# The gelu's VectorE work dealt over three steps, and waits of the heads' normalisation that pass in any step

## The chip, the cores and the metric

The kernel runs on 1 core of one Trainium2 chip. The metric is the device time of one execution in microseconds (us); of several executions the median is given. Lower is better.

## The reference, cut to what matters

One transformer block in its parallel form: with x of 2048 tokens by 640 channels and xn = layernorm(x),

```python
def _A_ref(x, wqkv, wo):            # 32 heads of 20 channels
    q, k, v = qkv of x @ wqkv
    p = softmax(q @ k.T * 20 ** -0.5)
    return (p @ v) @ wo
def _B_ref(x, w1, b1, w2, b2):
    y = _layernorm(x)
    h = gelu(y @ w1 + b1)           # tanh form, 1536 wide
    return h @ w2 + b2
return x + _A_ref(xn, wqkv, wo) + _B_ref(xn, w1, b1, w2, b2)
```

## The kernel before, in words

**Three stretches.** First the input is normalised, transposed and split into pairs of 16-bit numbers, and q, k and v are made (lines 162 to 590, to about 225 us of the trace). Then comes the long stretch of attention with the MLP woven in (to about 1260 us). The rest is the output projection.

**The attention stretch.** A pair of heads `g` and a half `hf` of the queries make one of 32 units, in the order of the list ORDER. A unit has two column blocks `cc` of 512 queries, and each of these runs over 16 key blocks `kb` in four groups of four (GRP). For each key block `scores` (line 674) makes two matmuls into a PSUM tile `s` (three buffers) and ScalarE's exp from there into a tile `p` (L682). For two of the four key blocks of a group, `rest` (line 689) lets VectorE write `low`, what `p` loses when it is cut to 16 bits (L694). Once per group `pv` (line 699) multiplies the tiles of the group *before* with the values: four matmuls per split block with the cut `p`, then four with the two `low` tiles of that group, then eight with the two whole tiles, all on L711. So the second `low` of a group is asked for by TensorE one group later.

**The fill.** Between the scores of key blocks 1 and 2 of each group, `other` (line 1062) puts some matmuls of the MLP: `layer1` (L913) makes a 128 by 2 by 256 tile `pu` of the hidden layer, `layer2` (L945) a tile `py` of the output. Both use the one buffer of the pool `psM`, so the next tile of either kind waits until VectorE has read the one before. The projection (L1024) follows the MLP in the same way.

**Steps.** What is to be done beside this on the other engines is written as generators, and `tick` (line 611) takes each one step further. `tick` is called twice per group, after the scores of key blocks 1 and 3. There are two lists. Each generator in `sides` goes on at every step: a gelu, an `addup`, the loads of the next unit's q and k (`load_stack`). Those in `patient` go on only when the step has no VectorE work of the others in it: a generator yields the VectorE work that it has just issued, in us, `tick` adds it up in `t`, and `if its is patient and t > 0: break` skips the whole list. `begin` runs a generator's first part at once, at the place where the fill has ended a tile, and its work counts for the next step.

**The gelu** (line 845), 48 times: at `begin` it reads `pu` from PSUM (L849) and adds the bias (L850). At the next step come a square (L853) and a multiply-add (L854), then a step with nothing, then tanh on ScalarE (L857), then three VectorE instructions at the fourth step (L859 to L861) that write `hT`.

**The heads' normalisation** (`finish`, line 764), twelve times: when two or three units of the same half are unloaded, the sums and the unnormalised outputs come back from DRAM into `lt` and `oa` (L774, L802). VectorE adds and inverts the sums (L810 to L817), they go out and come back spread over the heads as `rb` (L831). Then VectorE adds, multiplies, cuts and subtracts on `oa` (L835, L837, L839, L841), one instruction a step, and the result goes out (L842). This is done for two blocks of 512 columns, with bare `yield`s as waits for the transfers in between. All but those of the last groups of heads in the second half stand in `patient`, as does `scale_ahead` (line 871), which waits eight steps and then scales a row.

In each step, the generators in `sides` come first, then `patient`, and after the step VectorE gets the next `low`: the first `low` of a group after the step behind key block 1, the second after the step behind key block 3.

Of the kernel before, what the change touches and what calls it, by code (L numbers as in the profile page):

```python
# [42 lines left out]
def mha_mlp_kernel(tc, x, wqkv, wo, w1, b1, w2, b2, out):  # L43
# [4 lines left out]
    with (  # L48
# [544 lines left out]
        with ExitStack() as scope:  # L593
# [4 lines left out]

            sides, patient = [], []
            taken = [0.0]

            def begin(it):
# [6 lines left out]
            def tick():  # L611
                t, taken[0] = taken[0], 0.0
                for its in (sides, patient):
                    if its is patient and t > 0:
                        break
                    for it in list(its):
                        r = next(it, self_end)
                        if r is self_end:
                            its.remove(it)
                        else:  # L620
                            t += r or 0.0

# [113 lines left out]
            def dma(g, hf):  # L736

                return (nc.scalar if (g, hf) == ORDER[-1] else nc.sync).dma_start

            def unload(g, hf, ev):  # L740
# [9 lines left out]
                if g + 1 in ENDS:  # L750
                    fins.append(finish(g + 1 - UNITS[ENDS.index(g + 1)], g + 1, hf))
                    if len(fins) == 1:

                        (sides if hf == 1 and g + 1 >= TAIL else patient).append(finishing())

            fins, direct = [], []
            ready = [0, 0]

            def finishing():
                while fins:  # L760
                    yield from fins[0]
                    fins.pop(0)

            def finish(g0, g1, hf):
                nh, r0, r1 = 2 * (g1 - g0), 2 * g0 * DH, 2 * g1 * DH
                last = (g1 - 1, hf) == ORDER[-1]
                go = dma(g1 - 1, hf)
                w = 1024 if last else 512
                lt = m1.tile([P, 2, 64], F32, tag="lt", name="lt")
                n = checks.pop()  # L770
                yield
                gd = g1 - 1 if last else g1
                for p in range(2):
                    go(lt[: (gd - g0) * 32, p, :], lpart[p, hf, 2 * g0 : 2 * gd, :].rearrange("h (b t) -> (h b) t", t=64))  # L774
                    for a in range(2 if last else 0):

                        r = 64 * a + PAD + DH + VW * p
                        go(lt[(nh - 2 + a) * 16 : (nh - 1 + a) * 16, p, :],
                           direct[0][r : r + 1].rearrange("o c (b t) -> o (c b) t", t=64))
                for c0 in range(0, 1024, w):  # L780
                    cols = slice(hf * 1024 + c0, hf * 1024 + c0 + w)
                    if last:
                        o0, o1 = (ptp.tile([P, 2, 512], F32, tag="p", name="oa").rearrange("p c t -> p (c t)")
                                  for _ in range(2))
                        rb = o0

                        sel = [ptp.tile([P, 2, 512], F32, tag="p", name="sel").rearrange("p c t -> p (c t)")
                               for _ in range(2)]
                        for b0, t in zip((0, 8), sel):
                            nc.gpsimd.tensor_copy(  # L790
                                t[: nh * 16, : 8 * nh * DH].rearrange("p (b h d) -> p b h d", b=8, h=nh),
                                ident[: nh * 16, : nh * 16].rearrange("p (h b) -> p b h", b=16)[:, b0 : b0 + 8, :, None]
                                .to_broadcast([nh * 16, 8, nh, DH]))
                    else:
                        o = m1.tile([P, 2, 512], F32, tag="oa", name="oa")
                        o0, o1 = o[:, 0], o[:, 1]
                        rb = m1.tile([P, 512], F32, tag="rb", name="rb")
                    hl = o1.bitcast(F16).rearrange("p (s t) -> p s t", s=2)[: r1 - r0]
                    o0, o1, rb = o0[: r1 - r0], o1[: r1 - r0], rb[: r1 - r0]
                    rd = 2 * gd * DH - r0  # L800
                    for p, o in enumerate((o0, o1)):
                        go(o[:rd], opart[p, r0 : r0 + rd, cols])  # L802
                        for a in range(2 if last else 0):
                            q0 = 64 * a + PAD + VW * p
                            go(o[rd + a * DH : rd + (a + 1) * DH], direct[0][q0 : q0 + DH].rearrange("d c t -> d (c t)"))
                    if c0 == 0:
                        for _ in range(W1 if last else 4):
                            yield
                        l = lt[: nh * 16]
                        nc.vector.tensor_add(l[:, 0], l[:, 0], l[:, 1])  # L810

                        nc.vector.tensor_scalar(l[:, 1], l[:, 0], LO, None, ALU.is_ge, ALU.min,
                                                accum_out=good[: nh * 16, n : n + 1])
                        if not last:
                            yield
                        nc.vector.tensor_scalar(l[:, 0], l[:, 0], 1e-30, None, ALU.max)
                        nc.vector.reciprocal(l[:, 1], l[:, 0])  # L817
                        if not last:
                            go(linv[hf, 2 * g0 : 2 * g1, :].rearrange("h (b t) -> (h b) t", t=64), l[:, 1])
                        for _ in range(4 if last else 1):  # L820
                            yield
                    if last:

                        rb = psS.tile([P, 2, 512], F32, tag="s", name="rb")[: nh * DH]
                        for b in range(16):
                            nc.tensor.matmul(rb[:, b // 8, b % 8 * 64 : b % 8 * 64 + 64],
                                             sel[b // 8][: nh * 16, b % 8 * nh * DH : (b % 8 + 1) * nh * DH],
                                             l[:, 1], start=True, stop=True)
                        rb = rb.rearrange("p c t -> p (c t)")
                    for h in range(0 if last else nh):  # L830
                        go(rb[h * DH : (h + 1) * DH],  # L831
                           linv[hf, 2 * g0 + h : 2 * g0 + h + 1, c0 : c0 + w].to_broadcast([DH, w]))
                    for _ in range(W2 if last else 4):
                        yield
                    nc.vector.tensor_add(o0, o0, o1)  # L835
                    yield
                    nc.vector.tensor_mul(o0, o0, rb)  # L837
                    yield
                    nc.vector.tensor_copy(hl[:, 0], o0)  # L839
                    yield  # L840
                    nc.vector.tensor_sub(hl[:, 1], o0, hl[:, 0])  # L841
                    go(oscr[:, r0:r1, cols].rearrange("s d t -> d s t"), hl)  # L842
                ready[hf] += 1

            def gelu(ps, r2f, hT, f):
                u = m1.tile([P, 2, MC], F32, tag="u", name="u")
                w = m1.tile([P, 2, MC], F32, tag="w", name="w")
                scale_rows(r2f)
                nc.vector.tensor_mul(u, ps, r2f[:, None, :].to_broadcast([P, 2, MC]))  # L849
                nc.vector.tensor_add(u, u, b1t[:, f : f + 2, None].to_broadcast([P, 2, MC]))  # L850
                yield 1.2

                nc.vector.tensor_mul(w, u, u)  # L853
                nc.vector.scalar_tensor_tensor(w, w, 1.0 / 0.044715, u, ALU.add, ALU.mult)  # L854
                yield 1.2
                yield
                nc.scalar.activation(w, w, AF.Tanh, scale=0.7978845608028654 * 0.044715)  # L857
                yield
                nc.vector.scalar_tensor_tensor(u, w, 1.0, u, ALU.add, ALU.mult)  # L859
                nc.vector.tensor_scalar(hT[:, f : f + 2, 0, :], u, ch, None, ALU.mult)  # L860
                nc.vector.scalar_tensor_tensor(hT[:, f : f + 2, 1, :], u, ch, hT[:, f : f + 2, 0, :],  # L861
                                               ALU.mult, ALU.subtract)
                yield 1.7

            def scale_rows(r2f):

                if r2f in unscaled:
                    unscaled.remove(r2f)
                    nc.vector.tensor_scalar(r2f, r2f, f1, None, ALU.mult)

            def scale_ahead(r2f):
                for _ in range(8):
                    yield
                scale_rows(r2f)

            def addup(ps, xb, t0, hf):
# [121 lines left out]
            W1, W2 = 12, 9  # L998
# [56 lines left out]
            with tc.manual_schedule():  # L1055
# [18 lines left out]
                for g, hf, cc, kb0 in groups:  # L1074
# [23 lines left out]
                    if cc == 0 and kb0 == 0 and (g, hf) != ORDER[-1]:  # L1098
                        n = ORDER[ORDER.index((g, hf)) + 1]
                        sides.append(load_stack(*n, *([stacks[g, hf][1]] if n[0] == g else [])))  # L1100
                n = 0
# [119 lines left out]
```

## Time and profile before

| | us |
|---|---|
| median of 3 executions | 1363.1 (1362.19 to 1364.39) |
| the profiled execution's own time | 1364.71 |
| its span, from the first to the last instruction | 1363.0 |
| VectorE busy | 1060.5 |
| ScalarE busy | 1129.6 |
| mean granted TensorE clock | 0.998 |

The span is what the trace shows of one execution; 1.7 us of the device time lie around it. Busy times are unions over an engine's instructions. A wait in the trace is idle time of an engine just before an instruction, with the instruction or transfer that came last before it could start. A TensorE instruction's end is modelled, so idle time of TensorE is read with care. In rows of the timeline the columns are start, time from the first start to the last end, engine, line, operation, tiles and count; in square brackets stands the idle time before it and what ended it. VectorE is DVE there, TensorE PE, ScalarE ACT, and SPq is the queue from which SyncE issues transfers.

### The profile page before, as it was taken

The numbers are of one execution on the slowest core, as the hardware profiler recorded it, in microseconds if no ns is written. First come the engines' busy times: TensorE is split into PE (matmuls) and PEld (weight loads), VectorE is DVE, ScalarE is ACT, GpSimd is POOL, SyncE is SP. The second block draws the span as 40 slices with busy tenths as digits, with TensorE's granted clock in tenths as the row PEclk, the third lists the DMA queues.
The fourth block names the chain that finished last, engine by engine and source line by source line (L and its number), as shares of the span: only waits on it lengthen the run. The fifth ranks groups of instructions, "written<-read, shape, count | busy, mean of one in ns | idle before, by whom it ended". The sixth has DMA issues, their size and how long they took to land.

```text
span 1363.0 us, 29029 instructions
## 1 busy us (share of the span) xinstructions
PE 1335.1 (98%) x11651; PEld 591.6 (43%) x11651; DVE 1060.5 (78%) x1436; ACT 1129.6 (83%) x1305; POOL 30.2 (2%) x74
## 2 busy tenths in 40 slices
PE   9999999999999999999999999999999999999998
PEld 6545545443334334433433343434433333333465
DVE  6658835998779897978797789897879898888732
ACT  6654525999999999999999999999999999999700
POOL 2000000000000000000000000000000000000000
PEclk9999999999999999999999999999999999999999
DMA  9868731111113221212321141223032223244275
GB/s 269 270 157 154 146 101 57 34 52 43 48 58 94 62 83 60 52 50 84 93 71 51 37 109 48 86 62 86 19 87 85 70 81 86 59 135 118 88 233 175
DMA packets 103073, 127.94 MB, mean 94 GB/s; under 512 B 27516, under 2 KB 69568, under 8 KB 102932
## 3 DMA queue, kind: packets, MB, share of 16 engines
q1 hardware_dynamic: 99864, 119.60, 31.2%
q0 software_dynamic: 2304, 5.24, 2.4%
q8 instruction: 93, 1.52, 0.5%
q10 hardware_dynamic: 764, 1.18, 0.3%
q14 instruction: 48, 0.39, 0.1%
HBM read 80.50 MB, written 42.51 MB: 90 GB/s over the span
## 4 chain that ended last, share of the span: by engine, by line
PE 79%; DVE 9%; ACT 7%; issue 3%; DMA 2%; ACTq 0%; SPq 0%; DVEq 0%
PE o L711 26%; PE s L680 17%; PE py L945 11%; PE pu L913 9%; PE qkp L322 8%; PE vp L395 5%; ACT p L682 4%; PE z L1024 4%; DVE low L694 3%; DMA oa<-ev 1%; DVE u L849 1%; DMA qkscr<-qkhl 1%; DVE u L850 1%; DVE w L853 1%; DVE w L854 1%
## 5 line engine op out<-in xcount | busy, mean ns | idle before, releaser
L682 ACT ACTIVATE p<-s 128x1024 f32<-128x1024 f32 x1024 | 972.3, 1041 | 43.4 <-PE s L680 37.0
L694 DVE TENSOR_TENSOR low<-p 128x1024 f16<-128x1024 f32 x512 | 610.7, 1219 | 159.9 <-ACT p L682 159.7
L711 PE MATMUL o<-p,vfull 128*32 128x512 bf16 (+1 forms) x4096 | 430.8, 493 | 0.0
L680 PE MATMUL s<-qs,ks 61*128 61x512 f16 x2048 | 316.5, 382 | 7.4 <-ACT p L682 6.5
L680 PEld LDWEIGHTS <-ks 61*128 61x128 f16 x2048 | 63.7, 94 | 293.6 <-issue 291.3
L913 PE MATMUL pu<-xm,w1t 128*128 128x256 f16 x1440 | 179.3, 274 | 1.4 <-DVE u L849 1.4
L945 PE MATMUL py<-w2t,hT 128*128 128x320 f16 x1152 | 178.5, 300 | 1.5 <-DVE u L849 1.5
L913 PEld LDWEIGHTS <-w1t 128*128 128x128 f16 x1440 | 130.5, 98 | 68.8 <-issue 55.1
L945 PEld LDWEIGHTS <-hT 128*128 128x128 f16 x1152 | 102.4, 98 | 88.6 <-issue 54.3
L322 PE MATMUL qkp<-xnt,wv 128*128 128x512 f16 x600 | 132.7, 383 | 2.3 <-DVE qkhl L338 2.1
L711 PEld LDWEIGHTS <-vfull 128*32 128x32 f16 x3072 | 60.8, 95 | 139.8 <-issue 108.5
L711 PE MATMUL o<-low,vfull 128*32 128x512 f16 x1024 | 104.0, 378 | 4.3 <-DVE low L694 4.3
L322 PEld LDWEIGHTS <-wv 128*128 128x128 f16 x600 | 58.7, 99 | 73.2 <-issue 2.6
L711 PEld LDWEIGHTS o<-p,vfull 128*32 128x32 f32 x2048 | 62.6, 108 | 51.3
L337 ACT ACTIVATE qkhl<-qkp,qks 128x1024 f16<-128x1024 f32 (+1 forms) x24 | 23.2, 968 | 66.5 <-PE qkp L322 43.3
L1024 PE MATMUL z<-w1t,ot 128*128 128x320 f16 x480 | 66.7, 300 | 1.8 <-DVE oa L837 1.8
L395 PE MATMUL vp<-wv,xnt 128*128 128x320 f16 x480 | 66.7, 299 | 0.0
L338 DVE SCALAR_TENSOR_TENSOR qkhl<-qkp,qks,qkhl 128x1024 f16<-128x1024 f32 (+1 forms) x24 | 26.5, 1105 | 45.3 <-ACT qkhl L337 44.5
L1024 PEld LDWEIGHTS <-ot 128*128 128x128 f16 x480 | 46.3, 98 | 23.1 <-issue 2.9
L395 PEld LDWEIGHTS <-xnt 128*128 128x128 f16 x480 | 46.7, 98 | 18.7
L983 DVE SCALAR_TENSOR_TENSOR acc<-z,sc,acc 128x320 f32<-128x320 f32 x32 | 17.5, 550 | 43.2 <-PE z L1024 39.9
L732 ACT ACTIVATE ev<-o 128x512 f32<-128x512 f32 x64 | 39.2, 612 | 4.2 <-PE o L711 4.1
(179 smaller groups left out, 666.7 us busy)
## 6 DMA issues: line engine op xcount, KB each, us to landing
qkscr<-qkhl SPq DMA_DIRECT2D x40, 256.0 KB
opart<-ev SPq DMA_DIRECT2D x124, 80.0 KB
ks<-qkscr SPq DMA_DIRECT2D x120, 80.0 KB
qs<-qkscr SPq DMA_DIRECT2D x192, 40.0 KB
oa<-opart SPq DMA_DIRECT2D x32, 240.0 KB
xt<-in_A_x_dram SPq DMA_DIRECT2D x16, 320.0 KB
xscr<-xnt SPq DMA_DIRECT2D x4, 1280.0 KB
xm<-xscr SPq DMA_DIRECT2D x8, 640.0 KB
```

The costliest lines, as they stand in the source:

```text
L322: nc.tensor.matmul(ps[:, i, :], wv[:, k, q, a, mm * P : (mm + 1) * P], xnts[c][:, k, b, :], start=(k + n == 0), stop=(k == KD - 1 and n == 2))
L337: nc.scalar.activation(hl[:, 0, i0:i1], ps[:, i0:i1], AF.Copy, scale=a)
L338: nc.vector.scalar_tensor_tensor(hl[:, 1, i0:i1], ps[:, i0:i1], a, hl[:, 0, i0:i1], ALU.mult, ALU.subtract)
L395: nc.tensor.matmul(ps[:, hf, :320], xnts[c][:, k, a, j * P : (j + 1) * P], wv[:, k, 2, b, hf * 320 : (hf + 1) * 320], start=(n == 0), stop ...
L680: nc.tensor.matmul(ps[:, a, :], ks[64 * a : 64 * a + 61, kb * P : (kb + 1) * P], qs[64 * a : 64 * a + 61, cc * 512 : (cc + 1) * 512], star ...
L682: nc.scalar.activation(pt, ps, AF.Exp, scale=QS)
L694: nc.vector.tensor_sub(low, pt, upper(pt))
L711: nc.tensor.matmul(pv.o[32 * q : 32 * q + 32, :], src[:, v0 - PAD * (1 - q % 2) :][:, :32], t, start=q not in pv.begun, stop=last, skip_gr ...
L732: nc.scalar.activation(evs[g, hf][:, cc], pv.o, AF.Copy)
L913: nc.tensor.matmul(ps[:, i], w1v[:, k, (f + i) // 4, a, fo_ : fo_ + P], xnt[:, k, b, :], start=(n == 0), stop=(n == 3 * KD - 1))
L945: nc.tensor.matmul(ps[:, :320], hTs[mc][:, f, a, j * P : (j + 1) * P], w2v[:, f, b, hf * 320 : (hf + 1) * 320], start=(n == 0), stop=(n == ...
L1024: nc.tensor.matmul(ps[:, :320], ot[:, k, a, j * P : (j + 1) * P], wov[:, k, b, h * 320 : (h + 1) * 320], start=(n == 0), stop=(n == 3 * KD ...
```

## The change

Two edits.

*The gelu.* At `begin` only L849 is issued (0.6 is yielded). At the next step come L850 and L853 (1.2), at the step after it L854 (0.6), then tanh and the three others at the same steps as before. The number of instructions is the same.

*The list `patient`.* A generator that yields WAIT goes on at its next step whether or not the step has VectorE work. One that yields nothing is taken on only in a step with none. `waits(n)` is n steps of which the first n - 1 are such free ones; it replaces the bare loops in `finish` and in `scale_ahead`.

Set side by side, the programs of the two kernels have the same instructions in the same order on TensorE, ScalarE and GpSimd. On VectorE and in SyncE's queue the order differs: L854 of each gelu stands one `low` later, behind the second `low` of its group in place of ahead of it, and the instructions of the first ten of the twelve normalisations stand up to 12 `low`s earlier, those of `scale_ahead` up to 4. The last two normalisations stand where they stood, and so does everything behind them.

```diff
             sides, patient = [], []
+            WAIT = -1.0
+            free = set()
             taken = [0.0]
...
             def tick():
                 t, taken[0] = taken[0], 0.0
                 for its in (sides, patient):
-                    if its is patient and t > 0:
-                        break
                     for it in list(its):
+                        if its is patient and t > 0 and it not in free:
+                            continue
+                        free.discard(it)
                         r = next(it, self_end)
                         if r is self_end:
                             its.remove(it)
+                        elif r == WAIT:
+                            free.add(it)
                         else:
                             t += r or 0.0
...
+            def waits(n):
+                for _ in range(n - 1):
+                    yield WAIT
+                yield
+
...
                 n = checks.pop()
-                yield
+                yield WAIT
...
                     if c0 == 0:
-                        for _ in range(W1 if last else 4):
-                            yield
+                        yield from waits(W1 if last else 4)
                         l = lt[: nh * 16]
                         nc.vector.tensor_add(l[:, 0], l[:, 0], l[:, 1])
...
                         for _ in range(4 if last else 1):
-                            yield
+                            yield WAIT
...
-                    for _ in range(W2 if last else 4):
-                        yield
+                    yield from waits(W2 if last else 4)
                     nc.vector.tensor_add(o0, o0, o1)
...
                 nc.vector.tensor_mul(u, ps, r2f[:, None, :].to_broadcast([P, 2, MC]))
+                yield 0.6
                 nc.vector.tensor_add(u, u, b1t[:, f : f + 2, None].to_broadcast([P, 2, MC]))
+
+                nc.vector.tensor_mul(w, u, u)
                 yield 1.2
-
-                nc.vector.tensor_mul(w, u, u)
                 nc.vector.scalar_tensor_tensor(w, w, 1.0 / 0.044715, u, ALU.add, ALU.mult)
-                yield 1.2
-                yield
+                yield 0.6
                 nc.scalar.activation(w, w, AF.Tanh, scale=0.7978845608028654 * 0.044715)
...
             def scale_ahead(r2f):
-                for _ in range(8):
-                    yield
+                yield from waits(8)
                 scale_rows(r2f)
```

## The prediction, made before the changed kernel ran

> **What bounds the kernel now.** I read the page first, for the busy engines and the chain.
>
> ```profile
> PE 1335.1 (98%) x11651; PEld 591.6 (43%) x11651; DVE 1060.5 (78%) x1436; ACT 1129.6 (83%) x1305; POOL 30.2 (2%) x74
> PE 79%; DVE 9%; ACT 7%; issue 3%; DMA 2%; ACTq 0%; SPq 0%; DVEq 0%
> ```
>
> TensorE is busy nearly throughout and carries the chain. VectorE is idle for a fifth of the span and has 9% of the chain all the same, so TensorE waits for it now and then. Next the waits, for how often:
>
> ```profile
> PE s L680 <- ACT p L682: 6.5, 21, 1.2
> PE o L711 <- DVE low L694: 4.3, 8, 0.9
> PE py L945 <- DVE u L849: 1.5, 2, 0.9
> PE pu L913 <- DVE u L849: 1.4, 2, 0.8
> DVE oa L835 <- DMA oa<-ev: 2.7, 1, 2.7
> ```
>
> (Sum, times, longest.) In the attention stretch TensorE waits eight times for a `low` and four times until VectorE has emptied the fill's PSUM tile. VectorE itself waits for a transfer of the normalisation once, at the end of the kernel. Windows of 50 us show whether another engine stands as near to full:
>
> ```profile
> core 0: us, PE busy (x) PEld busy (x) DVE busy (x) ACT busy (x) POOL busy (x), PEclk, DMA share, GB/s
> 250.00:300.00 50.00, 48.40 (x461) 20.43 (x454) 46.91 (x56) 47.52 (x55) 0.00 (x0) 1.00 0.17 48
> 500.00:550.00 50.00, 49.76 (x468) 19.43 (x470) 38.54 (x42) 48.39 (x54) 0.85 (x1) 1.00 0.24 70
> 1050.00:1100.00 50.00, 48.17 (x457) 19.43 (x454) 43.66 (x55) 47.03 (x54) 0.85 (x1) 1.00 0.32 87
> ```
>
> The second window has no wait for VectorE, the first and third have four of the twelve. In those VectorE is busier, TensorE loses 1.6 to 1.8 us, and ScalarE loses too: 47.0 to 47.5 against 48.4. So a stall that VectorE causes reaches ScalarE, but ScalarE is within 3% of full itself.
>
> The stall is best seen in the timeline, in a group that has none and the next, that has one:
>
> ```profile
> 305.44 0.64 PE L711 MATMUL o<-p,vfull 128*32 128x512 bf16 x8
> 305.81 1.22 DVE L694 TENSOR_TENSOR low<-p 128x1024 f16<-128x1024 f32 x1
> 306.95 0.69 DVE L849 TENSOR_TENSOR u<-pu,r2f 128x512 f32<-128x512 f32 x1
> 307.09 0.61 PE L680 MATMUL s<-qs,ks 61*128 61x512 f16 x4
> 307.67 0.69 DVE L850 TENSOR_TENSOR u<-u,b1t 128x512 f32<-128x512 f32 x1
> 308.40 0.69 DVE L853 TENSOR_TENSOR w<-u 128x512 f32<-128x512 f32 x1
> 309.12 0.69 DVE L854 SCALAR_TENSOR_TENSOR w<-w,u 128x512 f32<-128x512 f32 x1
> 309.40 0.66 PE L711 MATMUL o<-p,vfull 128*32 128x512 bf16 x8
> 309.73 3.49 DVE L694 TENSOR_TENSOR low<-p 128x1024 f16<-128x1024 f32 x3
> 311.00 0.40 PE L711 MATMUL o<-low,vfull 128*32 128x512 f16 x3 [0.73 <-DVE low L694]
> 312.19 0.60 PE L680 MATMUL s<-qs,ks 61*128 61x512 f16 x4
> 312.31 0.60 ACT L732 ACTIVATE ev<-o 128x512 f32<-128x512 f32 x1 [0.49 <-PE o L711]
> ```
>
> VectorE makes the group's first `low` at 305.81, then four instructions of the gelu, and only then the second `low`, from 309.73, which TensorE waits for until 311.00.
>
> **The stall costs more than its row says.** From the first matmul of `pv` to the next scores it is 307.09 - 305.44 = 1.65 us without a stall and 312.19 - 309.40 = 2.79 with one: 1.14 us for a row of 0.73, so 0.4 lies outside the row. The Trainium skill, Perfetto Trace Analysis, section "Per-instruction lifecycle: what the profiler-reported window actually captures", says that the end of a TensorE instruction is estimated from its size and not observed. The two start-to-start times agree with that; by the idle rows alone the eight stalls would be 4.3 us in place of the sum below.
>
> **The change, part by part.**
>
> *The gelu.* L854 goes behind the second `low`, which so starts 309.73 - 309.12 = 0.61 to 0.72 us earlier (the spacing of two such instructions, 307.67 - 306.95 = 0.72, less the closer spacing ahead of a `low`). I take 0.7. The eight stalls together are 4.3 + 8 x 0.4 = 7.5 us. The shortest is this:
>
> ```profile
> 696.39 0.40 PE L711 MATMUL o<-low,vfull 128*32 128x512 f16 x3 [0.21 <-DVE low L694]
> ```
>
> It is 0.6 us by this count, and the others are 0.7 or longer, so seven shrink by 0.7 and one by 0.6: **5.5 us** less, and 2.0 remain. The instruction count is the same, and nothing is added to VectorE's work.
>
> What is late instead is L854, and with it tanh on ScalarE. It ends one `low` later (three in 3.49 us, 1.14 apart). In the group above L854 ended at 309.81 and tanh began at 311.18, 1.37 later. The narrowest place of the 48 is this:
>
> ```profile
> 1087.77 0.69 DVE L854 SCALAR_TENSOR_TENSOR w<-w,u 128x512 f32<-128x512 f32 x1
> 1089.72 0.63 ACT L857 ACTIVATE w<-w 128x512 f32<-128x512 f32 x1
> ```
>
> 1089.72 - 1088.46 = 1.26 us against 1.14: 0.1 is left. So I take nothing for tanh; if the cover were short by 0.2 at all eight crowded gelus, it would be 1.6 us on ScalarE.
>
> *The step of L854.* The step after the square had no VectorE work and now has. So `patient` has its working steps less often: per gelu one, with tanh, where there were two. This alone would make the normalisations longer; the other edit repays it.
>
> *The waits of the normalisation.* They now go by in any step, and the order of the programs shows the first ten normalisations up to 12 `low`s earlier. TensorE's order is the same, so no fill begins earlier, and the last two normalisations, on which the projection's end waits, don't move: **nothing** at the end. What it changes is beside which gelu a VectorE instruction of a normalisation falls. That bears on the four waits for L849, which look like this:
>
> ```profile
> 833.77 1.22 DVE L694 TENSOR_TENSOR low<-p 128x1024 f16<-128x1024 f32 x1
> 834.90 0.68 DVE L841 TENSOR_TENSOR oa<-oa 120x512 f16<-120x512 f32 x1
> 835.50 1.22 DVE L694 TENSOR_TENSOR low<-p 128x1024 f16<-128x1024 f32 x1
> 836.64 0.68 DVE L849 TENSOR_TENSOR u<-pu,r2f 128x512 f32<-128x512 f32 x1
> 837.38 2.06 PE L945 MATMUL py<-w2t,hT 128*128 128x320 f16 x14 [0.54 <-DVE u L849]
> ```
>
> At all four places the three last instructions of a gelu and two or three of a normalisation stand in the queue shortly before (here L839, then L841). In the new order one of the normalisation's has gone from there at three places, two at one; the others stay. Bounds: 0 if the queue is as full as before, 2.9 us if all four waits go. An instruction is 0.68 us (0.4 for L839), the waits 0.5 to 0.9, so I take half, **1.5 us**.
>
> *The added risk in these waits* is that VectorE, which takes its instructions in order, stands at L835 for a transfer and every `low` queues behind it. The closest places have four steps between L841 of one column block and L835 of the next. This distance stood in the program of before already, at one late normalisation, and the only wait of L835 there is the one at the end. The transfers:
>
> ```profile
> 436.54 0.36 SPq L842 DMA_DIRECT2D oscr<-oa  x1
> 439.04 0.78 SPq L802 DMA_DIRECT2D oa<-opart  x2
> ```
>
> The write takes 2.5 us until the loads are issued; with 0.8 to issue and another 2.5 to land (an estimate, by the write) it is 5.8. Four steps are two groups, and a group is about 4.1 us (309.40 - 305.44 = 3.96, a stall or an unload more), so 8.2 us: 2.4 to spare. I take 0.
>
> SyncE's queue gets the normalisation's transfers earlier between the loads of q and k. These aren't waited for by TensorE in any row above, and the share of the DMA is 0.17 to 0.32 in the windows. I take 0, with 1 us for the worst.
>
> *The sum on TensorE* is 5.5 + 1.5 = 7.0 us. Not all of it reaches the end. Where TensorE comes earlier, ScalarE must follow: in the stalled group TensorE lost 1.14 us, ScalarE waited 0.49 at its next instruction, under half. But it isn't full either, 48.4 of 50 us without stalls, and catches up over the next groups. Between 0.43 (0.49 of 1.14) and 1 I take three quarters: 7.0 x 0.75 = **5.3 us**. The profiled execution would go from 1364.7 to 1359.4; it stood 1.6 above the median of the runs, so the median goes from 1363.1 to **1357.8**.
>
> **The rivals.**
>
> *All of it goes.* The stalls vanish wholly with their pieces too short for a row, and ScalarE follows: 7.5 + 2.9 = 10.4 us, 1352.7. For it: the busier windows lose on both engines. Against it: the second `low` moves 0.7, and at the worst stall 0.9 + 0.4 are to be had.
>
> *ScalarE sets the pace.* Then TensorE arrives earlier and waits for a free tile `s`, and the row "PE s L680 <- ACT p L682" grows from 6.5 us by what the two others lose. Only part of ScalarE's own waits would be saved: 0.43 x 7.0 = 3.0 at most, and 1 if tanh comes late too and takes 0.25 us at each of the eight. It would be 1360.1 to 1362.1. For it speaks ScalarE's 48.4 of 50. The Trainium skill, Perfetto Trace Analysis, section "Identifying the Most-Contended Engine", calls occupancy a fair measure for ScalarE and matmul busy time a bad one for TensorE, and by that rule ScalarE would be the engine to judge by. Against it the trace has 37 us of this, most of it small waits in the stretch:
>
> ```profile
> ACT p L682 <- PE s L680: 37.0, 121, 1.3
> ```
>
> ScalarE still waits for TensorE far more often than the other way round.
>
> *Slower: the normalisation falls into the full queue.* Per gelu one step with tanh is left for it where there were two, and that step stands right ahead of the three last instructions (0.68 + 0.49 + 0.75), a `low` and the next L849. An instruction there adds up to 0.7 us to the queue, and where it is full already, a stall of 0.7 + 0.4 = 1.1 us on TensorE. The ten moved normalisations have eight such instructions each. With fewer than 7.0 / 1.1 = 6 of these 80 in a full queue the gain stands; from then on it is a loss, and with 10, 11.0 - 7.0 = 4 us, 1367. Against it: VectorE is a fifth idle, and only crowded gelus, eight or nine of 48, have a full queue; the order of the programs shows only one or two of the moved instructions newly there.
>
> *The change doesn't do what it says* would be L854 still ahead of the second `low`; the order of the program excludes it. That the waits are shorter but the ends of the normalisations aren't needed earlier, I already count as nothing.
>
> **How the numbers follow.** Forecast 0.55 (1355 to 1360), all of it 0.17, ScalarE's pace 0.18, slower 0.10. About 0.2% of this kernel, 2.7 us, is what a measurement tells from no change, so faster begins below 1360.4: the forecast and all of it are faster, 0.72; of ScalarE's pace I count the whole as the same, 0.18; slower 0.10. The range leaves out the slower case and the ends of two others: from 1352.5, just beyond all of it, to 1363.0.
>
> **What would show it.** Right: the wait for `low` falls from 4.3 us and eight times to under 1 us in the rows, those for L849 to about half; `pv` takes 1.65 us nearly everywhere; TensorE's busy time in the window from 250 to 300 comes near 49; no row of tanh waiting for VectorE; VectorE waits for `oa` only at the end. Wrong: a new row of VectorE waiting for a transfer of `oa` or `rb` in the stretch; a row "ACT w L857 <- DVE w L854" or whichever line it then has; or a wait of TensorE for ScalarE well above 6.5 us, with the time as before. It would also be wrong if the stretch ended earlier and the projection, whose order is the same, gave it back.

## The result, and the profile after

| | before | after |
|---|---|---|
| median of 6 executions | 1362.87 us | 1356.16 us (1355.62 to 1356.80) |
| ratio, 95% interval | | 0.995, 0.994 to 0.996 |
| the profiled execution's span | 1363.0 | 1354.4 |
| start to first exp | 223.4 | 221.0 |
| first exp to the end of the last | 1064.6 | 1059.0 |
| end of the last exp to the end | 75.0 | 74.4 |

The change takes 6.7 us. In the two profiled executions 5.6 us come from the attention stretch. The 2.4 us of the first stretch are no part of the change: no instruction differs there, and over the ten profiles of this study the first exp begins between 221.0 and 224.5 us. Part of it is the granted TensorE clock: from 46 to 50 us it is between 0.56 and 0.59 in before's profile and 1.00 in after's. Over the whole execution the two hardly differ, 0.998 and 0.999. A second set of executions beside a second set of before gave 1357.78 against 1363.09, 0.9961 (0.9948 to 0.9974).

The lines numbered after the diff differ: L694 of before is L700 after, L711 is L717, L849 is L858, L850 is L860, L853 is L862, L854 is L864, L835 is L844. The page's busy engines and its chain:

```profile
PE 1331.0 (98%) x11651; PEld 590.4 (44%) x11651; DVE 1055.9 (78%) x1436; ACT 1128.1 (83%) x1305; POOL 30.2 (2%) x74
PE 76%; DVE 9%; ACT 6%; DMA 5%; issue 2%; SPq 1%; ACTq 0%; DVEq 0%
```

Nothing is to be seen of the change here: shares of the span don't show a gain of half a per cent, and VectorE's 9% of the chain stay. The waits do (sum, times, longest):

```profile
PE s L686 <- ACT p L688: 7.5, 21, 2.1
DVE oa L844 <- DMA oa<-opart: 3.7, 3, 2.5
DVE oa L844 <- DMA oa<-ev: 2.2, 1, 2.2
PE py L953 <- DVE u L858: 1.5, 3, 0.7
PE pu L921 <- DVE u L858: 0.7, 1, 0.7
ACT p L688 <- PE s L686: 33.8, 108, 1.0
```

The row of `pv` waiting for `low` (4.3 us, eight times) has gone altogether. The waits for the emptying of the fill's tile fell from 2.9 to 2.2 us only, and there is a new row, VectorE waiting for `oa` inside the stretch. TensorE's wait for a free `s` grew from 6.5 us to 7.5, its longest from 1.2 to 2.1. That longest one is at 1217 us:

```profile
1200.88 0.97 SPq L985 DMA_DIRECT2D ot<-oscr  x2
1201.95 0.70 SPq L986 DMA_DIRECT2D acc<-accscr  x1
1202.75 1.09 SPq L634 DMA_DIRECT2D w1t<-in_A_wo_dram  x1
1214.81 0.74 ACT L640 ACTIVATE junk<-w1t 128x640 bf16<-128x640 f32 x1 [0.84 <-DMA w1t<-in_A_wo_dram]
1217.09 0.39 PE L686 MATMUL s<-qs,ks 61*128 61x512 f16 x2 [2.13 <-ACT p L688]
```

ScalarE stands 0.84 us for the load of the output weights, and the exps behind it are late. So it isn't ScalarE's work that grew. All five profiles with the freed waits of the normalisation have ScalarE waiting for this load, 0.3 to 0.8 us, and none of the other five. In the changed kernel two other loads of the projection, 1280 KB together, are issued just ahead of it (L985, L986). In e3 below, whose normalisations stand as before, those two are issued only at 1219 us. That they delay it is read from this order and wasn't tried alone.

The group that was shown before the change, now on VectorE and TensorE:

```profile
301.55 0.64 PE L717 MATMUL o<-p,vfull 128*32 128x512 bf16 x8
301.86 1.22 DVE L700 TENSOR_TENSOR low<-p 128x1024 f16<-128x1024 f32 x1
303.00 0.68 DVE L858 TENSOR_TENSOR u<-pu,r2f 128x512 f32<-128x512 f32 x1
303.72 0.69 DVE L860 TENSOR_TENSOR u<-u,b1t 128x512 f32<-128x512 f32 x1
304.44 0.69 DVE L862 TENSOR_TENSOR w<-u 128x512 f32<-128x512 f32 x1
305.05 1.22 DVE L700 TENSOR_TENSOR low<-p 128x1024 f16<-128x1024 f32 x1
305.46 0.64 PE L717 MATMUL o<-p,vfull 128*32 128x512 bf16 x8
305.93 0.79 PE L717 MATMUL o<-low,vfull 128*32 128x512 f16 x4
306.19 0.69 DVE L864 SCALAR_TENSOR_TENSOR w<-w,u 128x512 f32<-128x512 f32 x1
307.26 0.65 ACT L866 ACTIVATE w<-w 128x512 f32<-128x512 f32 x1
307.51 0.60 PE L686 MATMUL s<-qs,ks 61*128 61x512 f16 x4
```

The second `low` stands ahead of L864 now. `pv` takes 307.51 - 305.46 = 2.05 us, against 2.79 before and 1.65 without a stall: 0.4 us are still waited for, and there is no idle row for them. The first of the four matmuls with `low` starts in time and counts as busy for 0.38 us, and the three others start as it ends; the four make one entry of 0.79 us (0.39 where nothing is late). Tanh starts at 307.26, 0.38 after L864's end.

So that such hidden pieces count, I take all 256 `pv` of each profile, from the first matmul to the next one that isn't of `pv`, and add up what each is longer than the median (1.64 us). This sum, called **pv's lengthening** below, is 9.2 us before and 3.2 after.

The windows, with the columns as before:

```profile
250.00:300.00 50.00, 49.57 (x474) 21.04 (x473) 48.05 (x57) 48.29 (x57) 0.00 (x0) 1.00 0.21 58
1050.00:1100.00 50.00, 48.49 (x459) 19.97 (x452) 44.85 (x57) 46.87 (x54) 0.85 (x1) 1.00 0.36 101
```

From 250 to 300 us TensorE went from 48.40 to 49.57 busy and ScalarE from 47.52 to 48.29: the stalls there are nearly gone, and ScalarE took up what TensorE had. From 1050 on much is left.

### The profile page after: what moved, and what is told of

Its sections match the earlier page's. It is cut to its first block, busy times and chain, and to the rows that moved or that the text cites. A ratio compares the mean times of both kernels' runs of the same rounds, so it can differ in the third digit from the quotient of the medians.

```text
span 1354.4 us, 29034 instructions
## 1 busy us (share of the span) xinstructions
PE 1331.0 (98%) x11651; PEld 590.4 (44%) x11651; DVE 1055.9 (78%) x1436; ACT 1128.1 (83%) x1305; POOL 30.2 (2%) x74
## 4 chain that ended last, share of the span: by engine, by line
PE 76%; DVE 9%; ACT 6%; DMA 5%; issue 2%; SPq 1%; ACTq 0%; DVEq 0%
PE o L717 25%; PE s L686 16%; PE py L953 10%; PE pu L921 9%; PE qkp L322 7%; DVE low L700 4%; PE vp L395 4%; PE z L1032 4%; ACT p L688 3%; DMA qkscr<-qkhl 1%; DMA w1t<-in_A_wo_dram 1%; DMA oa<-ev 1%; DMA oa<-opart 1%; ACT wv L428 1%; DMA oscr<-oa 1%
## 5 line engine op out<-in xcount | busy, mean ns | idle before, releaser
L700 DVE TENSOR_TENSOR low<-p 128x1024 f16<-128x1024 f32 x512 | 614.3, 1218 | 154.7 <-ACT p L688 154.3
L717 PE MATMUL o<-p,vfull 128*32 128x512 bf16 (+1 forms) x4096 | 429.4, 493 | 0.0
L717 PEld LDWEIGHTS <-vfull 128*32 128x32 f16 x3072 | 59.6, 95 | 132.8 <-issue 102.0
L717 PE MATMUL o<-low,vfull 128*32 128x512 f16 x1024 | 102.1, 378 | 0.2
L717 PEld LDWEIGHTS o<-p,vfull 128*32 128x32 f32 x2048 | 62.2, 108 | 53.1
```

The lines of the kernel that those rows point to most:

```text
L700: nc.vector.tensor_sub(low, pt, upper(pt))
L717: nc.tensor.matmul(pv.o[32 * q : 32 * q + 32, :], src[:, v0 - PAD * (1 - q % 2) :][:, :32], t, start=q not in pv.begun, stop=last, skip_gr ...
```

## The experiments

They ran in two sets, each beside the kernel before: e1 to e4 (before: 1363.44), then the changed kernel again with e5 to e7 (before: 1363.09). One view of them all (us; the stretch is from the first exp's start to the last one's end; waits for L849 are the sum of the rows of `py` and `pu`):

| | ratio to before (95%) | pv's lengthening | waits for L849 | stretch | rest |
|---|---|---|---|---|---|
| before | 1 | 9.2 | 2.9 | 1064.6 | 75.0 |
| after | 0.995 (0.994 to 0.996) | 3.2 | 2.2 | 1059.0 | 74.4 |
| after, second set | 0.9961 (0.9948 to 0.9974) | 4.6 | 2.3 | 1059.2 | 74.4 |
| e1, gelu alone | 1.0042 (1.0025 to 1.0058) | 2.2 | 0 | 1060.3 | 83.1 |
| e2, waits alone | 0.9994 (0.9985 to 1.0003) | 9.9 | 1.3 | 1064.2 | 75.1 |
| e3, L854's place alone | 0.9959 (0.9945 to 0.9974) | 2.8 | 2.5 | 1058.2 | 74.3 |
| e4, low ahead of the step | 0.9952 (0.9936 to 0.9967) | 1.1 | 3.0 | 1057.3 | 74.3 |
| e5, and L849 ahead of low | 0.9941 (0.9928 to 0.9954) | 3.2 | 0 | 1055.9 | 74.2 |
| e6, square moved too | 0.9948 (0.9935 to 0.9961) | 2.1 | 2.3 | 1057.8 | 74.4 |
| e7, nothing held back | 1.0010 (1.0001 to 1.0018) | 9.7 | 2.4 | 1066.7 | 75.5 |

Of the 4.6 us of the second set 1.5 belong to one `pv` whose `low` had been ready for 4 us. It starts 0.3 us after a wait of 1.97 us for a free `s`, and the granted clock is half there. The first line is from this profile, the second from the first set's, where a wait of 2.13 us at the same place had no such sequel:

```profile
1219.00:1220.00 1.00, 1.00 (x12) 0.19 (x4) 1.00 (x2) 1.00 (x3) 0.00 (x0) 0.50 0.43 98
1219.00:1220.00 1.00, 0.81 (x9) 0.25 (x6) 0.89 (x1) 1.00 (x2) 0.00 (x0) 1.00 0.53 141
```

**e1: the gelu's part alone.**

```diff
 (before)
                 nc.vector.tensor_mul(u, ps, r2f[:, None, :].to_broadcast([P, 2, MC]))
+                yield 0.6
                 nc.vector.tensor_add(u, u, b1t[:, f : f + 2, None].to_broadcast([P, 2, MC]))
-                yield 1.2
-
                 nc.vector.tensor_mul(w, u, u)
+                yield 1.2
                 nc.vector.scalar_tensor_tensor(w, w, 1.0 / 0.044715, u, ALU.add, ALU.mult)
-                yield 1.2
-                yield
+                yield 0.6
```

> The gelu's part of the change alone; the waits of the normalisation as before. TensorE's order differs from before only where the projection starts, because the normalisations end later (each gelu leaves them one step where there were two). Theory of the place (what counts is that L854 stands behind the second low): the waits for low fall from 4.3 us to under 1, worth about 4 to 5 us, and the end loses what the later normalisations cost there, which I put at 0 to 4 us: 1358 to 1363. Theory of the normalisation (the gain comes from its earlier or other places): no gain, 1363 or slower. ScalarE's pace: 1361 to 1363.

It is slower than before, 1367.01 us against 1363.44. TensorE's order is that of before up to 1276 us of before, and there e1 is 9.7 us ahead of it, counted from the first exp: `pv`'s lengthening is 2.2 us, and no wait for L849 is left. No other kernel of the study is so far ahead at this place (the changed kernel is 5.6 us ahead, e3 6.3, e5 8.6). All of it and 3.8 us more are lost from there on. The last two exps come 5.7 us late, which leaves the stretch 4.3 us shorter than before's, and the rest is 8.1 us longer. The waits after 1270 us, of which before had 1.8 us for TensorE's `z` and 2.7 for `oa`:

```profile
DVE oa L835 <- DMA rb<-linv: 6.2, 1, 6.2
PE z L1024 <- DVE acc L983: 6.1, 2, 5.5
ACT p L682 <- PE s L680: 6.0, 1, 6.0
PE z L1024 <- DMA ot<-oscr: 4.2, 2, 3.7
```

The last normalisations ended late, the projection's order moved with them, and its matmuls wait for transfers and for sums that stand behind a VectorE waiting for `rb`. After these waits TensorE also ran slowly for some time:

```profile
1275.16 0.56 PE L1024 MATMUL z<-w1t,ot 128*128 128x320 f16 x2 [3.69 <-DMA ot<-oscr]
1301.95 4.16 PE L1024 MATMUL z<-w1t,ot 128*128 128x320 f16 x15 [5.49 <-DVE acc L983]
1302.00:1304.00 2.00, 2.00 (x8) 1.08 (x8) 1.89 (x7) 0.00 (x0) 0.00 (x0) 0.50 0.69 165
1312.00:1314.00 2.00, 2.00 (x17) 1.45 (x15) 1.64 (x3) 0.00 (x0) 0.00 (x0) 1.00 0.87 288
```

At a granted clock of 0.50 it makes 8 matmuls of the projection in 2 us, at 1.00 it makes 17. By this rate the 15 matmuls from 1301.95 and ten from 1276.20, which took 4.16 and 2.78 us, lost about 4 us (an estimate from these rows). So of some 13.5 us lost at the end, TensorE's waits for `z` are 8.5 more than before's and the halved clock about 4. My range for e1, 1358 to 1363, was too low: I had put the end at 0 to 4 us.

**e2: the waits' part alone** (the changed kernel with the gelu of before).

> The waits' part of the change alone; the gelu as before. Theory of the place: the eight waits for low stay at about 4 us and the gain is that of some waits for L849, 0 to 1.5 us: 1361 to 1363. Theory of the normalisation: most of the 6.7 us, below 1359. TensorE's and ScalarE's orders are those of before.

No difference that can be told, 1362.60 against 1363.44; the interval leaves room for 2 us. `pv`'s lengthening is 0.7 us longer, the waits for L849 have halved, and the stretch is 0.4 us shorter. The gain isn't that of the earlier normalisations.

**e3: the place of L854 alone.** As e1, but the last yield stays bare, so that the step of L854 isn't counted as VectorE work and the normalisations stand exactly where they stood.

```diff
 (e1)
                 nc.vector.scalar_tensor_tensor(w, w, 1.0 / 0.044715, u, ALU.add, ALU.mult)
-                yield 0.6
+                yield
```

> The gelu's part alone, but the step of L854 is not counted as VectorE work, so that the normalisations stand exactly where they stood before: the only difference in any engine's order is that L854 of each gelu stands one low later. Theory of the place: the waits for low fall below 1 us, pv's lengthening from 9.2 us to about 3, and the time falls by 4 to 6 us, to 1357 to 1359. ScalarE's pace: TensorE's wait for a free tile s grows by what the others lose and the time falls by less than 3, above 1360. Theory of the normalisation: 1362.9, no difference.

1356.62 against 1363.44. One instruction of each gelu, behind a `low` in place of ahead of it, gives as much as the whole change: the intervals of the two overlap. Its waits in the stretch:

```profile
PE s L680 <- ACT p L682: 6.5, 21, 1.2
PE py L945 <- DVE u L849: 1.3, 2, 0.7
PE pu L913 <- DVE u L849: 1.2, 2, 0.7
```

TensorE's wait for a free tile `s` is 6.5 us, as before: ScalarE didn't become the pace. Between e3 and e1 lies only the 0.6 that is yielded, and with it the place of the normalisations: 10.4 us at the end of the kernel, though e1 was 3.3 us ahead of e3 where the projection began.

**e4: the second low ahead of the step.**

```diff
 (before)
+                        if kb % GRP == 3:
+                            rest(units[1])
                         tick()
...
-                            for u in units[1:]:
+                            for u in units[2:]:
                                 rest(u)
```

> The kernel before, gelu and waits as they were, but the second low of each group is issued ahead of the step in place of behind it, so that no gelu or normalisation work of that step stands ahead of it. Theory of the place: all of pv's lengthening (9.2 us) goes, the waits for L849 stay: 6 to 9 us faster, 1354 to 1357. ScalarE's pace: no faster than the changed kernel, 1356 or above, with longer waits of TensorE for a free tile s.

1355.57 against 1363.44. The gelu is the one of before, and no work of the step stands ahead of the second `low` any more. `pv`'s lengthening is 1.1 us, and the waits for L849 (1.6 and 1.4) are what they were. The time is in the middle of what I expected of the place. It is only 0.4 us below what I expected if ScalarE set the pace, which decides nothing; but TensorE's wait for a free `s` is 6.5 us, as before, where that theory had it longer.

**e5: and L849 ahead of the first low.**

```diff
 (e4)
-                            rest(units[0])
                             credit += rate
                             other()
+                            rest(units[0])
```

> The kernel before with the second low of each group ahead of the step's work, and with the first low behind the fill, so that L849, which empties the fill's PSUM tile, stands ahead of the first low. Theory of the place: the last 3 us of waits for L849 go too, pv's lengthening stays near 1, and it is 1 to 3 us faster than with the second low alone: 1352.5 to 1355. Rival: VectorE now stands at L849 until the fill has ended while a low is ready behind it, the lows come late and pv lengthens by 3 us or more: 1356 or above. ScalarE's pace: 1355 to 1356, TensorE waits for a free tile s instead.

1354.83 against 1363.09, the lowest of the study; against e4 it isn't told apart, since the intervals overlap. Both the theory and its rival have part of it. VectorE's waits and TensorE's:

```profile
DVE u L849 <- PE pu L913: 44.8, 29, 2.8
PE s L680 <- ACT p L682: 6.6, 21, 1.2
ACT w L857 <- DVE w L854: 0.4, 1, 0.4
PE o L711 <- DVE low L694: 0.3, 1, 0.3
```

No wait for L849 on TensorE is left. VectorE now stands 44.8 us for the fill. Six `pv` are longer by 0.2 to 0.7 us, 2.5 of the 3.2 us. The standing isn't seen to cause them: just ahead of their lows VectorE works through gelu and normalisation instructions without a pause. The rival's sign, a lengthening of 3 us, came, but not by its mechanism.

**e6: the square behind the low as well.**

```diff
 (after)
                 nc.vector.tensor_add(u, u, b1t[:, f : f + 2, None].to_broadcast([P, 2, MC]))
+                yield 0.6
 
                 nc.vector.tensor_mul(w, u, u)
-                yield 1.2
                 nc.vector.scalar_tensor_tensor(w, w, 1.0 / 0.044715, u, ALU.add, ALU.mult)
-                yield 0.6
+                yield 1.2
```

> The changed kernel with the square (L853 of the kernel before) moved behind the second low as well, in one step with the multiply-add; the normalisations stand as in the changed kernel. Theory of the place: the remaining 3.2 us of pv's lengthening fall to 1 or less, worth 2 us, 1354 to 1355.5, as long as tanh doesn't wait. The cover of tanh: the multiply-add now ends 0.7 us later still, where 0.1 us was left at the narrowest place, so tanh should wait for VectorE at the eight crowded gelus, 0.2 to 0.6 us each, 2 to 4 us on ScalarE, which gives back the gain: 1356 to 1358.

1355.98 against 1363.09, between what the two expected. `pv`'s lengthening falls to 2.1, the stretch is 1.2 us shorter than after's, and no row shows tanh waiting for VectorE. The cover of tanh wasn't at its end, as I had thought. In its own set it is 1.8 us below the changed kernel, and the intervals of the two overlap, so the gain isn't told apart.

**e7: nothing held back.**

```diff
 (after)
                     for it in list(its):
-                        if its is patient and t > 0 and it not in free:
-                            continue
                         free.discard(it)
```

> The changed kernel with no holding back at all: the normalisations and the row scalings take a step at every step, also where the gelu has VectorE work. Theory of the full queue (the slower rival): more of the eighty instructions fall beside a crowded gelu, pv lengthens by more than the 3.2 us of the changed kernel and waits for L849 by more than 2.2, together 2 to 6 us more, and VectorE waits for oa or rb more often: 1357 to 1362. Rival (VectorE has a fifth of its time to spare, so where they fall doesn't matter): 1356.2, no difference.

Slower than the changed kernel by more than was expected, 1364.39 against before's 1363.09 and after's 1357.78. `pv`'s lengthening is 9.7 us again, and two things make it up. Nearly half, 4.3 us, is one place, where VectorE stands for a transfer and the `low` behind it is late:

```profile
1072.58 0.69 DVE L842 TENSOR_TENSOR oa<-oa 120x512 f32<-120x512 f32 x1 [5.18 <-DMA oa<-opart]
1073.19 1.22 DVE L698 TENSOR_TENSOR low<-p 128x1024 f16<-128x1024 f32 x1
1074.46 0.57 PE L715 MATMUL o<-low,vfull 128*32 128x512 f16 x3 [2.95 <-DVE low L698]
```

(L842 is L835 of before, L698 its L694.) Of the 4.3 us, 2.95 are this wait; the granted clock is 0.51 from 1076 to 1078 us, and the eight f32 matmuls of this `pv` take 2.26 us where 1.03 is usual. The rest is in nine other `pv` of 0.2 to 1.0 us and in smaller pieces; at those that were looked at (426, 441 and 831 us) an instruction of a normalisation stands between the gelu's and the late `low`. So the holding back that the change keeps for working steps is worth 6.6 us, as much as the whole gain.

## Why the prediction was right, point by point

The forecast was 1357.8, the time 1356.16 and 1357.78 in two sets: the direction, the place and the size held. That the size came so near is partly luck: two terms and a zero of the sum were off, and they made up for one another.

- **The second low.** Foretold: seven stalls shorter by 0.7 and one by 0.6, 5.5 us, with 2.0 left. Measured: the eight are 7.4 us long before and 1.5 after, 5.9 less; in all `pv`'s lengthening fell by 6.0 to 3.2. The 1.8 us beside the eight are four shorter ones (0.85 us together) and pieces below 0.1 us. That the stall costs more than its row, 0.4 us each, was needed: by the rows alone, 4.3 us, the gain of e3 and e4 couldn't be had. e3 shows the cause by itself.
- **The waits for L849.** Foretold 1.5 us of 2.9, about half, as a sign of being right; measured 0.7. Two of the four went, two stayed and two new ones came, beside other gelus. This term was over-sized: I had looked only where waits had been, not where moved instructions would make some. Against e3, whose normalisations stand as before, the moved ones bring nothing: waits for L849 and `pv`'s lengthening are 5.4 us together in the changed kernel and 5.3 in e3.
- **The share that reaches the end.** Foretold three quarters. In the experiments that gained, the stretch falls by nearly all that TensorE waits less: after 5.6 of 6.7, e3 6.4 of 6.8, e4 7.3 of 8.0, e6 6.8 of 7.7, e5 8.7 of 8.9, which is 0.84 to 0.98; the second set 5.4 of 5.2, and e1 9.7 of 9.9 up to the place where its order parts. ScalarE follows almost wholly, and TensorE's wait for a free `s` is 6.5 to 7.5 us in all of these but e1. This term was under-sized, and it made up for the one above.
- **SyncE's queue.** I took 0, with 1 us for the worst. The worst came: the longest wait for a free `s` is 2.13 us in place of 1.17 at this place in e3, for the load of the output weights. This is about what the changed kernel's share falls short of e3's.
- **The normalisations.** That the waits' part gives nothing by itself is shown by e2. That it repays what the counted step of L854 costs was said without a price; e1 gives it: about 13.5 us at the end, against some 3 us that e1's later normalisations bring in the stretch (9.7 us ahead where e3 is 6.3). The sentence that this edit is worth nothing at the end is right only against before. Within the change it is what keeps the gelu's part from being a loss.
- **The slower rival** named a mechanism that is there: in e7 normalisation instructions in the full queue lengthen several `pv`. But nearly half of e7's lengthening is VectorE standing for a transfer and the slow clock after it, so e7 doesn't show the full queue deciding alone. In the changed kernel the two new waits for L849 and a new lengthening of 0.4 us at 446 us, which e3 doesn't have, come with the moved normalisations.
- **Tanh.** No row of tanh waiting for VectorE came, as foretold. Its lateness shows on the other side: VectorE waits for tanh 3.9 us in 15 places where it was 1.4 in eight, and no row has TensorE waiting for it.
- **The transfer's cover failed.** A new row of VectorE waiting for `oa` in the stretch was one of my signs of being wrong, and it came: 3.7 us at three places. I had counted 2.5 us for the write, 3.3 for the loads, and 2.4 to spare. The changed kernel at one such place:

```profile
477.90 0.68 DVE L850 TENSOR_TENSOR oa<-oa 120x512 f16<-120x512 f32 x1
478.61 0.35 SPq L851 DMA_DIRECT2D oscr<-oa  x1
482.99 0.77 SPq L813 DMA_DIRECT2D oa<-opart  x2
487.24 0.69 DVE L844 TENSOR_TENSOR oa<-oa 120x512 f32<-120x512 f32 x1 [2.54 <-DMA oa<-opart]
487.85 1.22 DVE L700 TENSOR_TENSOR low<-p 128x1024 f16<-128x1024 f32 x1
```

The write took 482.99 - 478.61 = 4.4 us and the loads another 4.3 to VectorE's start, 8.6 in place of 5.8. VectorE stood 2.5 us. It cost TensorE nothing there: no `pv` near it is longer than the median by 0.1 us; e7 shows such a wait where it did. Over the ten profiles 104 of 110 such writes took 2.0 to 2.9 us and six 3.3 to 4.4. Where VectorE stood for the loads of 2 x 240 KB, these took 3.9 to 6.1 us, so the loads were under-priced at every such place and the write at few. That before's program had the same distance once without a wait was no proof that it is enough.

What held this write up can be seen in the trace's packets, of which the changed kernel has these from 480.9 to 483 us (packets, MB, share of 16 engines):

```profile
q8 instruction: 1, 0.02, 2.9%
q1 hardware_dynamic: 4, 0.00, 1.0%
```

By 481.0 us all but the last 2 KB of the 240 have gone. Then a packet of 16 KB of instructions takes 0.97 us from 480.98, and the last two packets of the write come at 481.93 and 482.04, as it ends. Of the six late writes four have such a packet among their own, and the two others share their time with 128 packets of another transfer. Of the 104 others 18 have an instruction packet too, most of them ahead of their data or at its end. That this packet delays the write is read from the order in time; no run was made without it.

*What stays open:* Not tried were a version with e5's order and longer waits, and one that holds the normalisations back as e1 does but lets the last ones through in time; either might be faster than any here.

## What to carry to other kernels

When a saturated engine waits now and then for one that has time to spare, look at what stands ahead of the late result in the spare engine's order. Moving one instruction of 0.7 us behind it gave as much as the whole change here, and issuing the wanted result first (e4) needs no dealing at all. A rule that lets background work pass only in free steps couples everything: counting 0.6 us more in one step gained 3 us in the stretch and cost over 13 at its end, 10 us net, so price what such a rule delays, up to the last consumer. And look at the granted clock behind a long wait of the busy engine before the whole loss is put down to the wait.

## What the runs showed of the hardware that was not expected

A stall of TensorE inside a run of small matmuls on column groups shows only in part as idle time: 0.73 us in the row, 1.14 from start to start, and 0.4 us with no row at all after the change. At seven places ahead of the last 20 us of the ten profiles the granted clock is 0.50 for 3.4 or 6.8 us, each time from within a wait of TensorE of 1.6 to 5.5 us or from up to 0.8 us behind it. In 2 us eight matmuls of the projection then run in place of 17. Waits of 1.6 to 2.1 us without this are in the profiles too, so what decides it stays open. The way of 240 KB out to DRAM and of 2 x 240 KB back took 8.6 us at 478 us, where at 436 us of before the write alone took 2.5 in place of 4.4; a 16 KB packet of instructions of 0.97 us stands ahead of the late write's last two packets.
